# Moving the small score matmuls to the end of a visit that covers two pairs of heads

## The chip, the cores and the metric

The kernel runs on one core of a Trainium2 chip. The metric is the time on the device of one execution, in microseconds (us); of several executions the median is taken. The engines are named as the profile names them: PE (TensorE, its matmuls), PEld (TensorE's loads of stationary weights), DVE (VectorE), ACT (ScalarE), POOL (GpSimd) and SP (SyncE, which here only starts transfers). PSUM has eight banks of 128 partitions by 512 float32 values, and matmuls write there.

## What is computed

Blockwise causal attention over 8 batches, 8 heads, 576 positions and 64 values per head, followed by a feed-forward layer with a swish gate:

```python
block = 64
scores = matmul(q, k.transpose(0, 1, 3, 2)) / sqrt(64)
scores = where(pos[:, None] // block >= pos[None, :] // block, scores, -1e9)
attn = exp(scores - max) / sum
x = matmul(attn, v)              # then reshaped to 4608 rows by 512
h = x @ w_in                     # 512 by 2048
g = h * (1 / (1 + exp(-beta * h)))
out = g @ w_out                  # 2048 by 512
```

A query sees the keys of its own block of 64 positions and of all earlier blocks. In tiles of 128 keys, the scores are a staircase: key tile 0 needs all 576 queries, tile 1 the queries from 128 on, and so on; the last key tile has only 64 keys and the last 64 queries.

## The kernel before

Two heads form a pair, of which there are 32, four to a batch. In a pair, one head's 64 values lie in partitions 0 to 63 and the other's in partitions 64 to 127, so the score matmuls of the two heads use the two row halves of the array and run beside each other. Scores are computed transposed, keys in PSUM's partitions, queries along the free dimension.

The scores of one pair fall into four groups, and the table `blocks` in the function `fq` lists them (key tile, first query, last query, offset in the bank):

- group 0: key tile 0 with queries 0 to 511
- group 1: key tile 0 with the last 64 queries, and key tile 1 with 448 queries
- group 2: key tile 2 with 320 queries, and key tile 3 with 192 queries
- group 3: key tile 4, which has 64 keys and 64 queries: a matmul of 64x64 for each head

Groups 0 to 2 write to a pair of PSUM banks each (tile class `PP`), one bank for each head, with all 128 columns of the array; this is the form 64*128 in the profile. Group 3 writes to partitions 0 to 63 for one head and 64 to 127 for the other, of one shared bank (`small`, of class `P1`), and uses 64 rows by 64 columns of the array for each: the form 64*64.

A *visit* is one operation of the plan in which PE computes some of these groups without a break. For batches 0 and 1 a visit covers one pair of heads. For batches 2 to 7 (`JOIN`), two pairs, `u` and `u + 1`, share three visits: groups 0 and 1 of the first pair; groups 2 and 3 of both; groups 0 and 1 of the second pair. There are twelve visits of the middle kind in a run, with twelve matmuls each. All the work in a visit has one set of waits ahead of it, and its last instruction raises the semaphore that ACT waits for.

After a visit ACT computes the exponentials (L724 for groups 0 to 2, 128x1024 values each; L736 for group 3), DVE clears the upper blocks of the staircase (L730, L732), PE multiplies with the values (L764), DVE normalizes (L776, L783) and the result is transposed to `xT`, by PE for the first batches and by a transposing DMA on SP's queue (L800) for the later ones. Q and K arrive by DMA in `ST`, POOL casts them to bfloat16 in `QKn` (L665), and a second transposing DMA (L672) makes `QKT`, which the visits read.

The feed-forward layer runs on nine chunks of 512 rows: PE multiplies with `w_in` (L1000), ACT takes the tanh (L1010), DVE forms the gate (L1014), and PE multiplies with `w_out`, plainly for the first chunk (L1036) and in seven products of quarters for the others (L921). Filler matmuls (L523, L525) keep PE occupied near the start.

The order on every engine is made before the program is built. A planner, the class `Plan`, simulates the engines with durations that are written at each operation, takes the ready operation with the lowest priority value, assigns buffers and PSUM banks, and writes one fixed queue for each engine; `assign` then derives the semaphore waits. Visits are spread through the feed-forward work in this way. The planner sees a visit as a single operation of fixed duration and doesn't look at the order of the matmuls in it. That order is written out by hand: `fq` walks the list `visits` entry by entry, for each entry its blocks, and for each block the two heads.

Of the kernel before, what the change touches and what calls it, by code (L numbers as in the profile page):

```python
# [359 lines left out]
def bass_blockwise_causal_attn__then__act_swish_beta_kernel(  # L360
# [10 lines left out]
    with es:  # L371
# [66 lines left out]
        def pr(u):  # L438
            b, c = divmod(u, NPAIR)
            return u if b < 1 else 10 * u if b < 2 else 994 + 100 * (b - LAG) + 4.9 * c  # L440
        def again(g, o, i, x):

            return g.add_instruction(mybir.InstMatmult(
                start_tensor_calc=True, stop_tensor_calc=True, tile_size=i.tile_size, tile_position=i.tile_position,
                ldweights=False, name=nc.get_next_instruction_name(), engine=i.engine,
                ins=[g.lower_ap(x), i.ins[1]], outs=[g.lower_ap(o)]))
# [154 lines left out]
        for u in range(NU):  # L601
# [77 lines left out]
            if b not in JOIN or p == 0:  # L679
                tes = {uu: P.tile("EX" if uu == 3 else "E") for uu in ((u,) if b not in JOIN else (u, u + 1))}  # L680
                qks = {uu: {} for uu in tes}
                visits = [[(u, g) for g in grp] for grp in GROUPS[b]] if b not in JOIN else [
                    [(u, 0), (u, 1)], [(u, 2), (u, 3), (u + 1, 2), (u + 1, 3)], [(u + 1, 0), (u + 1, 1)]]
                for grp in visits:
                    small = P.tile("P1") if any(g0 == 3 for _, g0 in grp) else None
                    pst = [P.tile("PP") if g0 < 3 else small for _, g0 in grp]

                    def fq(g, e, pst=pst, grp=grp, tqk=tqk, b=b):
                        keep = {}
                        for (uu, g0), ps in zip(grp, pst):  # L690

                            held = g0 == 1 and (uu, 0) in grp
                            blocks = {0: [(0, 0, 512, 0)], 1: [(0, 512, 576, 448), (1, 128, 576, 0)],
                                      2: [(2, 256, 576, 0), (3, 384, 576, 320)], 3: [(4, 512, 576, 0)]}[g0]
                            for t, q0, q1, off in blocks:
                                m = min(128, 576 - 128 * t)
                                for h in range(2):
                                    r = slice(64 * h, 64 * h + 64)
                                    if g0 < 3:
                                        o = PS[0:m, ps.slot + h, off:off + q1 - q0]  # L700
                                    else:
                                        o = PS[r, ps.slot, 64 * (uu % 2):64 * (uu % 2) + 64]
                                    y = 64 * h * (b >= QB)
                                    x = QKT[tqk.slot][r, uu % 2, 0, q0 + y:q1 + y]
                                    if held and t == 0:
                                        z = again(g, o, keep[h], x)
                                        continue
                                    z = g.matmul(o, QKT[tqk.slot][r, uu % 2, 1, 128 * t + y:128 * t + m + y], x)  # L708
                                    if t == 0:
                                        keep[h] = z.ins  # L710
                        return z

                    n = sum(220 if g0 < 3 else 60 for _, g0 in grp)
                    o = P.op("PE", n, fq, deps=cps, tiles=list({id(x): x for x in pst}.values()) + [tqk] + [tes[uu] for uu in sorted({uu for uu, _ in grp})] * (b > 0),
                             lat=n + 200, mode="row", prio=pr(u) + .2 if len(grp) == 4 else pr(u + 1) + .1 if grp[0][0] > u else
                             pr(u) + .1 + .1 * (grp[0][1] >= 2))
                    for (uu, g0), ps in zip(grp, pst):
                        qks[uu][g0] = o, ps
# [411 lines left out]
```

The softmax here doesn't subtract the row's maximum and nothing guards it: scores larger than these inputs give would overflow.

## Time and profile before

| what | before |
|---|---|
| median of 3 runs | 334.65 us (332.92 to 335.12) |
| span of the profiled execution | 330.9 us |
| the profiled execution's own time around its span | not on the page; median less span is 3.75 us |
| PE busy, of the span | 323.5 us |
| DVE busy / ACT busy | 221.8 us / 212.6 us |
| score matmuls of L708, form 64*128, 320 columns | 64, mean 306 ns |
| score matmuls of L708, form 64*128, 192 columns | 64, mean 243 ns |
| score matmuls of L708, form 64*64, 64 columns | 64, mean 212 ns |
| weight loads of L708, form 64*64 | 64, mean 103 ns |

The span runs from the first to the last instruction. A row of the profile such as "L708 PE MATMUL PS<-QKT 64*128 64x320" gives the line of the kernel, the engine, the operation, the written and the read tile, the rows and columns of the array in use, and the size of the moving operand. Matmuls overlap one another, so the mean duration of a row isn't what the matmul costs PE; the distance from one start to the next is nearer to it. The arrow at the end of a line names what ended the idle time ahead of an instruction.

### The profile page before, as it was taken

How to read it: one execution, taken by the hardware profiler on the slowest of the kernel's cores; microseconds unless marked ns; L12 is line 12 of the kernel's file. 1: busy time of each engine (PE TensorE's matmuls, PEld its weight loads, DVE VectorE, ACT ScalarE, POOL GpSimd, SP SyncE). 2: the span in 40 equal slices, each digit the busy share in tenths (PEclk: the TensorE clock that was granted, in tenths of full speed). 3: DMA queues.
4: the chain of work that ended last, by engine and by line, in shares of the span. 5: the costliest groups of instructions: out<-in, count | busy, mean ns of one | idle time of the engine just before them, and what ended most of it. 6: DMA issues, size and time to landing. Idle time of an engine off the chain costs nothing.

```text
span 330.9 us, 7510 instructions
## 1 busy us (share of the span) xinstructions
PE 323.5 (98%) x3145; PEld 204.2 (62%) x3089; DVE 221.8 (67%) x448; ACT 212.6 (64%) x324; POOL 84.6 (26%) x127
## 2 busy tenths in 40 slices
PE   7998999999999999999999999999999999999996
PEld 4574455445586457754765666576566766666685
DVE  4747875679754897358966695678467685666742
ACT  2876974297558886768657866974975555544521
POOL 7665081073073044104621530320000000000000
PEclk9999999999999999999999999999999999999999
DMA  7999999999999999979999999974102310110023
GB/s 214 229 239 234 192 234 198 187 293 200 202 268 190 207 247 198 229 158 216 204 176 224 199 240 214 200 152 80 35 34 40 92 45 34 60 37 32 3 95 127
DMA packets 154993, 53.41 MB, mean 161 GB/s; under 512 B 139072, under 2 KB 154448, under 8 KB 154960
## 3 DMA queue, kind: packets, MB, share of 16 engines
q1 hardware_dynamic: 141200, 40.19, 63.9%
q0 software_dynamic: 5568, 4.36, 8.3%
q10 hardware_dynamic: 8192, 8.39, 8.1%
q8 instruction: 24, 0.39, 0.5%
q14 instruction: 9, 0.07, 0.1%
HBM read 36.71 MB, written 9.44 MB: 139 GB/s over the span
## 4 chain that ended last, share of the span: by engine, by line
PE 92%; ACT 2%; DMA 2%; issue 1%; DVE 1%; SPq 1%; POOL 0%
PE PS L1000 38%; PE PS L921 30%; PE PS L708 9%; PE PS L764 8%; PE PS L1036 4%; DMA ST<-in_k_dram 2%; PE PS L525 1%; PE PS L813 1%; ACT E L724 1%; PE PS L634 1%; ACT xq L788 1%; SPq L618 1%; ACT th L1010 0%; POOL QKn L625 0%; DVE xq L783 0%
## 5 line engine op out<-in xcount | busy, mean ns | idle before, releaser
L1000 PE MATMUL PS<-xT,w_in 128*128 128x512 bf16 x576 | 136.6, 379 | 0.1
L1010 ACT ACTIVATE th<-PS,beta 128x512 f32<-128x512 f32 x144 | 96.5, 699 | 59.8 <-PE PS L1000 59.1
L1014 DVE SCALAR_TENSOR_TENSOR gT<-th,PS 128x512 f16<-128x512 f32 x144 | 95.1, 681 | 31.7 <-ACT th L1010 31.1
L724 ACT ACTIVATE E<-PS 128x1024 bf16<-128x1024 f32 x93 | 92.1, 1028 | 27.0 <-PE PS L708 27.0
L1000 PEld LDWEIGHTS PS<-xT,w_in 128*128 128x128 bf16 x576 | 53.4, 98 | 55.5 <-DVE gT L1014 1.8
L921 PE MATMUL PS<-w_out,gT 128*128 128x256 f16 x512 | 63.1, 273 | 0.0
L921 PEld LDWEIGHTS PS<-w_out,gT 128*128 128x128 f16 x512 | 49.0, 98 | 12.1 <-issue 1.5
L574 POOL CAST Vn<-Vs 128x640 bf16<-128x640 f32 (+1 forms) x28 | 21.6, 770 | 94.3 <-DMA Vs<-in_v_dram 93.1
L665 POOL CAST QKn<-ST 128x640 bf16<-128x640 f32 x48 | 36.7, 764 | 25.1 <-DMA ST<-in_q_dram 12.9
L708 PE MATMUL PS<-QKT 64*128 64x320 bf16 (+4 forms) x328 | 36.4, 297 | 0.4 <-ACT E L736 0.2
L764 PEld LDWEIGHTS PS<-Vn,E 128*128 128x128 bf16 x930 | 30.9, 97 | 3.9 <-issue 0.4
L942 ACT ACTIVATE ost<-PS 128x512 f32<-128x512 f32 x32 | 19.4, 606 | 21.5 <-PE PS L921 21.5
L921 PE MATMUL PS<-OV 128*128 128x256 f16 x256 | 31.9, 273 | 0.0
L764 PE MATMUL PS<-Vn,E 128*128 128x65 bf16 x930 | 31.8, 193 | 0.0
L708 PEld LDWEIGHTS PS<-QKT 64*128 64x128 bf16 (+1 forms) x328 | 13.4, 96 | 26.4 <-issue 11.6
L921 PEld LDWEIGHTS PS<-OV 128*128 128x128 f16 x256 | 24.2, 98 | 5.8 <-issue 1.1
L783 DVE TENSOR_TENSOR xq<-PS,inv 128x640 bf16<-128x640 f32 x30 | 24.6, 822 | 0.7
L885 DVE TENSOR_TENSOR OV<-gT 128x1024 f16<-128x1024 f16 x32 | 23.8, 753 | 1.1 <-PE PS L921 0.6
L730 DVE MEMSET E<- 64x64 uint32 x62 | 6.9, 112 | 22.5 <-ACT E L724 20.4
L945 DVE SCALAR_TENSOR_TENSOR ost<-PS,ost 128x512 f32<-128x512 f32 x22 | 15.1, 688 | 8.7 <-PE PS L921 6.2
L921 PE MATMUL PS<-OV,gT 128*128 128x256 f16 x128 | 16.1, 273 | 0.0
L1036 PE MATMUL PS<-w_out,gT 128*128 128x512 f16 x64 | 15.5, 380 | 0.0
(65 smaller groups left out, 176.2 us busy)
## 6 DMA issues: line engine op xcount, KB each, us to landing
out_dram<-ost ACTq DMA_DIRECT2D x32, 256.0 KB, 3.8
ST<-in_q_dram SPq DMA_DIRECT2D x12, 576.0 KB, 5.4
ST<-in_k_dram SPq DMA_DIRECT2D x12, 576.0 KB, 7.6
Vs<-in_v_dram SPq DMA_DIRECT2D x24, 256.0 KB, 4.3
ST<-in_q_dram SPq DMA_DIRECT2D x8, 288.0 KB, 6.3
ST<-in_k_dram SPq DMA_DIRECT2D x8, 288.0 KB, 6.5
w_in<-in_moe_w_in_dram POOLq DMA_DIRECT2D x4, 512.0 KB, 10.5
w_out<-in_moe_w_out_dram POOLq DMA_DIRECT2D x4, 512.0 KB, 9.5
```

The source lines that it names most:

```text
L574: return g.tensor_copy(Vn[t.slot][:, 0:n, g0:g1, 0:64], Vs[ts.slot][:, 0:n, g0:g1, :])
L665: return g.tensor_copy(QKn[tn.slot][:].rearrange("p a w n -> p (a w n)")[:, 640 * (2 * a + w):][:, 0:640] .rearrange("p (t h d) -> p t h d ...
L708: z = g.matmul(o, QKT[tqk.slot][r, uu % 2, 1, 128 * t + y:128 * t + m + y], x)
L724: return g.activation(E3[es_(te)][:, g0, :, :], PS[:, ps.slot:ps.slot + 2, :], ACT.Exp, scale=0.125)
L764: z = g.matmul(o, eblk(te, t, i, h), Vn[Tv.slot][:, t, 2 * c + h, 0:65], start=(t == 0), stop=(t == i))
L783: return g.tensor_tensor(xq[xq_(tx)][:].rearrange("p i (h d) -> p h i d", h=2), both(pv, 0, 64), x, ALU.mult)
L885: return P.op("DVE", dve_t(SZ * HC / 2), mk(lambda g: g.tensor_tensor(fo(), fx(), fy(), op)), deps=deps, tiles=tiles, prio=prio)
L921: x = g.matmul(PS[:, pw.slot, HM * w:HM * w + HM], fa()[:, j, 128 * w:128 * w + 128], fb()[:, j, :], start=first and (pair or w == 0) and ...
L1000: z = g.matmul(PS[:, ph.slot, :], w_in[:, c, 128 * j:128 * j + 128], xT[:, c, row % RX:row % RX + RC], start=(c == 0), stop=(c == 3))
L1010: return g.activation(th[tt.slot][:], PS[:, ph.slot, :], ACT.Tanh, scale=beta[:, j:j + 1])
L1014: return g.scalar_tensor_tensor(out=gT[tg.slot][:, j, :], in0=th[tt.slot][:], scalar=1.0, in1=PS[:, ph.slot, :], op0=ALU.add, op1=ALU.mult)
L1036: z = g.matmul(PS[:, po.slot, 0:d1 - d0], gT[tg.slot][:, j, 128 * w:128 * w + 128], w_out[:, j, d0:d1], start=(j == 0), stop=(j == NJ - 1))
```

## The change

In the middle visit of two pairs of heads, the list of groups is put in another order. Before, it goes through groups 2 and 3 of the first pair and then groups 2 and 3 of the second; afterwards through group 2 of both pairs and then group 3 of both. The set of matmuls, the tiles they read and write and the first and last instruction of the visit are unchanged.

```diff
-                    [(u, 0), (u, 1)], [(u, 2), (u, 3), (u + 1, 2), (u + 1, 3)], [(u + 1, 0), (u + 1, 1)]]
+                    [(u, 0), (u, 1)], [(u, 2), (u + 1, 2), (u, 3), (u + 1, 3)], [(u + 1, 0), (u + 1, 1)]]
```

For each visit this turns the sequence of pairs of matmuls (one for each head) from 320, 192, 64x64, 320, 192, 64x64 into 320, 192, 320, 192, 64x64, 64x64. The number 64x64 stands for the form 64*64, the others for the columns of the form 64*128.

## The prediction

> **What bounds the kernel now.** I read the page's head and busy slices first, then the chain that ended last, then three stretches of the span, and then TensorE's (PE's) timeline inside one of the twelve visits that the diff touches.
>
> ```profile
> span 330.9 us, 7510 instructions
> PE 323.5 (98%) x3145; PEld 204.2 (62%) x3089; DVE 221.8 (67%) x448; ACT 212.6 (64%) x324; POOL 84.6 (26%) x127
> PE   7998999999999999999999999999999999999996
> DMA  7999999999999999979999999974102310110023
> PE 92%; ACT 2%; DMA 2%; issue 1%; DVE 1%; SPq 1%; POOL 0%
> ```
>
> PE is busy in every slice, and the chain that ended last runs along PE for 92% of the span. DMA looks as full as PE until about slice 26 (215 us), so whether PE or the transfers set the pace has to be read from the waits. The stretch from 100 to 260 us, which holds ten of the twelve visits (the others start at 76.42 and 90.38), answers it. The columns are the stretch, its length, and the busy time of PE, weight loads, DVE, ACT and POOL:
>
> ```profile
> 60.00:100.00 40.00, 39.81 (x342) 22.68 (x330) 28.38 (x59) 25.71 (x39) 15.71 (x20) 1.00 1.16 231
> 100.00:260.00 160.00, 160.00 (x1622) 100.22 (x1581) 111.64 (x228) 117.20 (x175) 37.36 (x48) 1.00 0.88 168
> ```
>
> From 100 to 260 us PE is busy 160.00 of 160 us at the full granted clock; the next engine, ACT, has 27% to spare. Of PE's waits in the whole span, which sum to 4.3 us, none is for a transfer. So a nanosecond taken off PE's instruction stream there should come off the end.
>
> Busy time says nothing of how well the time is used, since matmuls overlap. Therefore the timeline of the visit at 119.39 us, put together from short windows of it (start, time, engine, line, tiles, count):
>
> ```profile
> 119.39 0.31 PE L708 MATMUL PS<-QKT 64*128 64x320 bf16 x2
> 119.54 0.25 PE L708 MATMUL PS<-QKT 64*128 64x192 bf16 x2
> 119.72 0.22 PE L708 MATMUL PS<-QKT 64*64 64x64 bf16 x2
> 119.72 0.11 PEld L708 LDWEIGHTS PS<-QKT 64*64 64x64 bf16 x2 [0.21 <-issue]
> 119.86 0.11 PEld L708 LDWEIGHTS PS<-QKT 64*128 64x128 bf16 x3
> 120.01 0.24 PE L708 MATMUL PS<-QKT 64*128 64x192 bf16 x2
> 120.19 0.22 PE L708 MATMUL PS<-QKT 64*64 64x64 bf16 x2
> 120.34 0.39 PE L1000 MATMUL PS<-xT,w_in 128*128 128x512 bf16 x1
> ```
>
> Read the starts, not the durations: 119.39, 119.54, 119.72, 119.86 (the second pair of heads' 320-column matmuls start with those loads), 120.01, 120.19, and 120.34 for the next work. The four 64x64 matmuls are short, yet the steps around them are long, and the load of 64x64 weights appears only at 119.72, after a hole of 0.21 us on the load side; nothing is loaded ahead across the change of form.
>
> The same trace shows what a small pair costs where its neighbours have its own form. Early in the span, a 64x64 pair stands between filler matmuls that are 64x64 as well:
>
> ```profile
> 16.85 0.19 PE L708 MATMUL PS<-QKT 64*64 64x64 bf16 x2
> 16.88 0.28 PE L525 MATMUL PS<-identF,identB 64*64 64x256 bf16 x2
> ```
>
> There the successor starts 0.03 us later (29 ns in the records), and its weights are already loading at 16.85.
>
> **What the Trainium skill says.** (1) "TensorEngine Tiling (Array Packing)", Key Properties: a change of tiling mode, as opposed to a change of tile, drains TensorE. The trace agrees and gives the size, about 95 ns, worked out below. (2) The same page, Restrictions under Tile-to-Partition Mapping: column tiling switches off Fast Weight Load. It agrees: a 64x128 weight load is followed by the next of its row half after 15 ns (119.390 to 119.405), while a 64x64 one needs about 29 (16.606 to 16.635). (3) "TensorE: Matmul & The Clock Gate", The mechanism: loads that go to the background weight buffer are pulled ahead of running matmuls. It agrees within one form (load for the 192-column pair at 119.405, under the 320-column pair), not across forms. (4) "Perfetto Trace Analysis", Tensor Engine Instruction: a matmul's end is estimated by the profiler. So I use starts alone.
>
> **The change, part by part.** It swaps two entries of one list. A visit's operation remains one operation with the same waits; its last instruction, which carries the semaphore, is still the second pair of heads' 64x64 matmul. The planner sees the same duration, and in the built program the queues of ACT, DVE, POOL and SP hold the same instructions in the same order; PE differs only inside twelve visits. No DMA, no wait, no instruction is added or removed. What is moved is one 64x64 pair with its two weight loads, past four wide matmuls and their loads.
>
> Rates: back-to-back 512-column matmuls of L1000 start 216 ns apart, 0.42 ns a column. So 320 columns stream in 134 ns, 192 in 81, 64 in 27.
>
> Before, by the records to the nanosecond at 119.39 us: 320 pair 147, 192 pair 174, small pair 149, and again 146, 176, 149 to L1000. Sum 0.94 us; eleven of the twelve visits run 0.94 (one 0.96). Against the rates, 192 to small is 174 - 81 = 93 above, small to wide 149 - 27 = 122 above (98 of switch and 24 of the exposed load: the small matmuls are recorded as 213 ns here, 189 where the load was hidden), and wide 320 is 147 - 134 = 13 above (its load).
>
> After: 320 pair 147; 192 pair to the second 320 pair, same form, load ahead, 81; second 320 pair, 134; second 192 pair to the small form 174; first small pair to the second 29, as at 16.85; second small pair to the next form 149. The exposed load of 24 is counted once in that 149 and is now the first pair's. Sum 714 ns. Saving: 943 - 714 = 229 ns a visit: two switches (93 + 98) and two exposed loads (24 + 13), times 12 = 2.75 us.
>
> Both ends of what isn't seen in this setting: if the second 320 pair still shows its load (+13), the 192 pair an equal one (+12), and the second small pair has to wait for its slow load (+26, as the 29 ns of load come after the first pair's), the visit takes 765 and the saving is 178 ns, 2.1 us in all. If the second small pair costs nothing beside the first, it is 258 ns, 3.1 us. A loss inside the visit I exclude: each step of the new order occurs in the old one or is bounded by one that does.
>
> What lies on the path: all of it, as PE doesn't idle from 100 us on. What becomes late next are the PE operations that arrive with little lead over ACT or DVE. By the semaphore times, ACT begins its exponentials at the end of every visit within 0.02 us, so they move up with it and carry what follows. Three L1000 operations and one L764 have leads of only 0.06, 0.11, 0.16 and 0.13 us over the DVE release they need (219.7, 225.9, 255.2 and 139.9 us). If those releases don't move, 0.17 + 0.12 + 0.07 + 0.10 = 0.46 us is lost there. I take a little under half, 0.2. Transfers: the shortest lead of a transposed Q/K tile is 2.3 us (visit at 175.26, by when seven visits will have saved 1.6); the last xT transposes lead L1000 at 267.15 by 1.4 us, but were issued after PE's own attention product at 261.02, so they move too.
>
> Net 2.55 us: the profiled span goes from 330.9 to about 328.3. Its own time outside the span isn't on the page; the median of the runs, 334.65, is 3.75 above the span, and I carry that over: **332.1 us**, 0.8% less.
>
> **The rivals.**
>
> A, forecast: full saving passed on, 332.1 (331.5 to 332.6 by the bounds). For: no PE idle. Chance 0.70.
>
> B, given back in waits: the visit shortens, but a reader of the small waits is right more often than I am; ACT, at 73% in the stretch, and DVE, at 70%, hold up PE after half the visits. 2.75 / 2 = 1.4 us left, 333.3. For: leads under 0.3 us follow five visits. Against: ACT waits for PE (27.0 us for visits alone), not the reverse. Chance 0.15.
>
> C, the order doesn't matter: the 0.1 us belongs to a small matmul as such, wherever it stands (two row halves writing one PSUM bank, say). Then 334.6. Against: 29 ns at 16.85, and the 64-column pair of L443, 28 ns in the wide form. That the new order isn't made at all is ruled out by the built program. Chance 0.07.
>
> D, slower: PE runs ahead of the transposed Q/K tiles while DMA is full. They take 4.9 to 12.3 us to land, typically 7.0. Should shifted timing turn a typical landing into the longest for a tile with 2.3 us of lead, PE stands 12.3 - 7.0 - 2.3 = 3.0 us; two such make 6.0, less 2.55 gained: +3.5, 338.1. It decides from 2.55 us of such waits in all (5.9 to show as slower). For: the DMA row. Against: eleven of the twelve landings lead by over 3 us, and PE waits for none now. Chance 0.06; 0.02 for others.
>
> **How the numbers follow.** About 1% (3.35 us) is what a measurement of this kernel can tell from no change; the three runs shown spread by 2.2 us. Case A lies within 1%; only its upper bound with the spread in its favour crosses, 0.12 in all. Slower is D. So faster 0.12, same 0.82, slower 0.06. The range takes A's bounds with half the spread of the runs on the low side, 330.9, and reaches over B to 334.0.
>
> **What would show it.** In the visits: starts 0.08 us after the first 192 pair for the second 320 pair, one hole on the load side instead of two, the four small matmuls in one group, a visit of about 0.71 us, the 64x64 row's mean nearer 200 ns than 212. PE still busy 160 of 160 us. Wrong if visits stay at 0.94 (C), if PE shows new waits for ACT or DVE after them (B), or for QKT transposes (D).

## The result: 0.4% less, where 0.8% was forecast

| | before | after |
|---|---|---|
| median of 20 runs | 334.2 us | 332.96 us |
| ratio of after to before | | 0.9959, 95% interval 0.9938 to 0.9981 |
| span of the profiled execution | 330.9 us | 330.6 us |
| its own time | not on record | 332.43 us |

The ratio is a gain of 1.4 us (0.6 to 2.1). The two medians, of all runs, are 1.2 us apart; the ratios, and the means of runs given below, leave out runs that took over 1.5% more than the fastest of their kernel. The time lies in the stated range of 330.9 to 334.0, and within 1% as was thought likeliest. It lies there because that range reached over rival B as well: the forecast itself was a gain of 2.55 us, which is outside the interval of the measured one. The question for the experiments is where the rest is.

The head of the page of the changed kernel, with the lines that answer to those shown of before (the granted clock added):

```profile
span 330.6 us, 7476 instructions
PE 319.7 (97%) x3111; PEld 204.3 (62%) x3089; DVE 221.6 (67%) x448; ACT 212.6 (64%) x324; POOL 85.9 (26%) x127
PE   6897999999999999999999999999999999999996
PEclk9997999999999999999999999999999999999999
PE 89%; ACT 2%; DVE 2%; DMA 2%; issue 2%; SPq 1%; POOL 0%
```

The two spans differ by 0.3 us alone, and it would be wrong to read the change's worth from them: this execution has something that the profiled execution of before has not. In slice 4 (25 to 33 us), long before the first of the twelve visits, PE had less than the full clock. Also, 34 matmuls fewer are on the page than before, all of L1000 (542 of 576): these are missing records. Most are the first of a row of L1000, and there the records show PE idle for 50 to 160 ns. Twenty of them lie between 100 and 260 us, and that is why the stretches (their length, then busy PE, PEld, DVE, ACT, POOL) show 158 us where before had 160:

```profile
60.00:100.00 40.00, 39.82 (x336) 22.77 (x330) 30.49 (x59) 23.76 (x37) 17.36 (x20) 1.00 1.09 229
100.00:260.00 160.00, 158.23 (x1619) 101.41 (x1598) 110.89 (x231) 119.20 (x178) 36.84 (x48) 1.00 0.92 170
```

PE's timeline of the visit that answers to the one shown of before, again put together from short windows:

```profile
121.10 0.31 PE L708 MATMUL PS<-QKT 64*128 64x320 bf16 x2
121.24 0.38 PE L708 MATMUL PS<-QKT 64*128 64x192 bf16 x4
121.33 0.38 PE L708 MATMUL PS<-QKT 64*128 64x320 bf16 x4
121.46 0.39 PE L708 MATMUL PS<-QKT 64*128 64x192 bf16 x4
121.64 0.25 PE L708 MATMUL PS<-QKT 64*64 64x64 bf16 x4
121.64 0.14 PEld L708 LDWEIGHTS PS<-QKT 64*64 64x64 bf16 x4 [0.21 <-issue]
121.82 0.39 PE L1000 MATMUL PS<-xT,w_in 128*128 128x512 bf16 x1
```

(The count in a line is of what overlaps the window, so take starts alone.) The second pair's 320 columns start 0.09 us after the first pair's 192, at 121.33, where a change of form took 0.17. The four small matmuls are one group with one hole of 0.21 us on the load side, not two. The visit runs from 121.10 to 121.82: 0.72 us, where it ran 0.94. The groups of small matmuls and their loads, first of before and then of after (count, then busy time and mean ns of one, then the idle time ahead):

```profile
L708 PE MATMUL PS<-QKT 64*64 64x64 bf16 x64 | 6.9, 212 | 0.0
L708 PEld LDWEIGHTS PS<-QKT 64*64 64x64 bf16 x64 | 3.4, 103 | 6.3 <-issue 6.3
L708 PE MATMUL PS<-QKT 64*64 64x64 bf16 x64 | 4.7, 204 | 0.0
L708 PEld LDWEIGHTS PS<-QKT 64*64 64x64 bf16 x64 | 2.5, 104 | 3.8 <-issue 3.8
```

So inside the visits the change did what was forecast. Two more facts stand in the records of both traces. From one end of a PE operation to the next, by the semaphore that PE raises, after gains on before exactly twelve times by 0.22 us, at the twelve visits, and nowhere from 60 us to the end does it lose more than 0.04. And the first visit begins at 78.73 us in this execution and at 76.42 in the one of before. The whole of the saving, 2.6 us, is in the stretch that the change touches, and 2.3 us were lost ahead of it.

### The profile page after: what moved, and what is told of

Same layout as the page of the kernel before. It is cut to its first block, busy times and chain, and to the rows that moved or that the text cites. A ratio compares the mean times of both kernels' runs of the same rounds, so it can differ in the third digit from the quotient of the medians.

```text
span 330.6 us, 7476 instructions
## 1 busy us (share of the span) xinstructions
PE 319.7 (97%) x3111; PEld 204.3 (62%) x3089; DVE 221.6 (67%) x448; ACT 212.6 (64%) x324; POOL 85.9 (26%) x127
## 4 chain that ended last, share of the span: by engine, by line
PE 89%; ACT 2%; DVE 2%; DMA 2%; issue 2%; SPq 1%; POOL 0%
PE PS L1000 36%; PE PS L921 29%; PE PS L708 8%; PE PS L764 8%; PE PS L1036 4%; DMA ST<-in_k_dram 2%; PE PS L525 1%; PE PS L813 1%; ACT E L724 1%; PE PS L634 1%; DVE gT L1014 1%; ACT xq L788 1%; SPq L618 1%; DVE xq L783 0%; ACT th L1010 0%
## 5 line engine op out<-in xcount | busy, mean ns | idle before, releaser
L1000 PE MATMUL PS<-xT,w_in 128*128 128x512 bf16 x542 | 130.9, 381 | 2.7 <-issue 0.5
L1000 PEld LDWEIGHTS PS<-xT,w_in 128*128 128x128 bf16 x576 | 53.4, 98 | 55.9 <-issue 2.2
L921 PE MATMUL PS<-w_out,gT 128*128 128x256 f16 x512 | 63.0, 273 | 0.0
L921 PEld LDWEIGHTS PS<-w_out,gT 128*128 128x128 f16 x512 | 48.9, 98 | 12.2 <-issue 1.5
L665 POOL CAST QKn<-ST 128x640 bf16<-128x640 f32 x48 | 37.9, 789 | 28.4 <-DMA ST<-in_k_dram 14.9
L708 PE MATMUL PS<-QKT 64*128 64x512 bf16 (+4 forms) x328 | 34.2, 297 | 0.4 <-ACT E L736 0.2
L921 PE MATMUL PS<-OV 128*128 128x256 f16 x256 | 32.0, 273 | 0.0
L921 PEld LDWEIGHTS PS<-OV 128*128 128x128 f16 x256 | 24.2, 98 | 5.7 <-issue 1.1
L885 DVE TENSOR_TENSOR OV<-gT 128x1024 f16<-128x1024 f16 x32 | 23.9, 753 | 1.1 <-PE PS L921 0.6
L921 PE MATMUL PS<-OV,gT 128*128 128x256 f16 x128 | 16.1, 273 | 0.0
L642 DVE COPY QKT<-PS 128x576 bf16<-128x576 bf16 x16 | 12.0, 756 | 5.8 <-PE PS L634 5.6
```

Of the source, the lines that this page charges most:

```text
L665: return g.tensor_copy(QKn[tn.slot][:].rearrange("p a w n -> p (a w n)")[:, 640 * (2 * a + w):][:, 0:640] .rearrange("p (t h d) -> p t h d ...
L885: return P.op("DVE", dve_t(SZ * HC / 2), mk(lambda g: g.tensor_tensor(fo(), fx(), fy(), op)), deps=deps, tiles=tiles, prio=prio)
L921: x = g.matmul(PS[:, pw.slot, HM * w:HM * w + HM], fa()[:, j, 128 * w:128 * w + 128], fb()[:, j, :], start=first and (pair or w == 0) and ...
L1000: z = g.matmul(PS[:, ph.slot, :], w_in[:, c, 128 * j:128 * j + 128], xT[:, c, row % RX:row % RX + RC], start=(c == 0), stop=(c == 3))
```

## The experiments

Two theories were held against each other. **Theory P**: what PE saves in the visits, 2.65 us, passes to the end in full, and what is missing from the medians is scatter ahead of the first visit. **Theory W**: about half is taken back by new waits after the visits. Each kernel was timed in five rounds against the kernel before. For each one profile was taken, and read in three stretches. A visit is measured from its first start to the start of what follows it. Single visits read 0.02 to 0.04 us more than the table has, and one of after's 0.95, by a missing record.

| kernel | visit, us | first visit at | first to last visit | last visit to end | half clock at 28 to 33 us | ratio to before (95%) |
|---|---|---|---|---|---|---|
| before | 0.94 | 76.42 | 173.42 | 81.06 | no | |
| before, copy (e1_null) | 0.94 | 78.56 | 173.39 | 81.07 | yes | 0.9999 (0.998 to 1.0018) |
| before, copy (e9_null) | 0.94 | 78.37 | 173.39 | 81.06 | yes | 1.001 (0.999 to 1.003) |
| after | 0.72 | 78.73 | 171.03 | 80.84 | yes | 0.9959 (0.9938 to 0.9981) |
| after (e2_after) | 0.72 | 78.75 | 171.11 | 80.83 | yes | 0.995 (0.9923 to 0.9976) |
| after (e8_after) | 0.72 | 78.28 | 171.90 | 80.84 | yes | 0.9949 (0.9925 to 0.9973) |
| half the visits (e3_half) | six 0.72, six 0.94 | 76.39 | 172.45 | 81.06 | no | 0.998 (0.9954 to 1.0005) |
| sixteen small pairs more (e4_pad) | 1.23 | 78.61 | 176.51 | 81.34 | yes | 1.01 (1.0061 to 1.0139) |
| small ones first (e5_first) | 0.72 | 79.16 | 171.62 | 80.84 | yes | 0.9984 (0.9962 to 1.0006) |
| six changes of form (e6_six) | 1.05 | 78.00 | 174.56 | 81.16 | yes | 1.0033 (1.001 to 1.0056) |
| after, early fillers (e10_fill_after) | 0.72 | 77.62 | 171.46 | 80.84 | no | 0.9946 (0.9928 to 0.9964) |
| before, early fillers (e11_fill_before) | 0.94 | 77.48 | 176.76 | 81.06 | no | 1.0036 (1.0017 to 1.0056) |

In the diffs below three dots mark lines left out. They are against the changed kernel; that of the six changes of form is against the kernel before, and the fillers went into both.

**The kernel before, copied, twice.** No edit.

> The kernel before, unchanged, against itself. Theory P (what PE saves in the twelve visits reaches the end in full, and the missing half lies in the scatter of the first 76 us, where nothing was changed): the ratio's interval holds 1.000; the stretch from the first of the twelve visits to the last is 173.4 us again within 0.3, while the start of the first visit moves by a microsecond or more against 76.42 us. Theory W (half of the saving is taken back by waits): says nothing of this run but that the first visit starts near 76.4 us again within 0.3, since the stretch before it does not scatter.

> The kernel before a second time, unchanged, beside it. Ratio's interval holds 1.000; the stretch of half clock in about 4 of 10 runs; first visit to last 173.4 us; the first visit near 76.4 us without that stretch in the profile, near 78.6 with it.

Both ratios hold 1.000, the middle stretch is the same to 0.03 us both times, and the first visit moves by 2.1 and 2.0 us. The half clock was in 7 and 8 of 22 runs. So the scatter is ahead of the visits, and the middle stretch is a clean measure of an edit to the visits. The larger part of the move comes with the stretch of half clock. The windows of the first copy's profile (length, busy PE, PEld, DVE, ACT, POOL, then the granted clock):

```profile
24.60:28.05 3.45, 2.04 (x37) 1.62 (x34) 2.79 (x8) 1.68 (x7) 3.23 (x4) 1.00 1.19 213
28.05:31.46 3.41, 3.37 (x20) 1.63 (x19) 1.45 (x2) 0.85 (x3) 1.65 (x2) 0.50 1.19 251
```

For 3.41 us PE runs at 0.50 of its clock, after a stretch in which it was busy 2.04 us of 3.45. In every profile with this stretch the first visit starts between 78.0 and 79.2 us, and in the two without it or the early fillers at 76.4. By the ends of PE's operations against those of before, 1.2 to 1.4 us of each move arise from 27 us on, with the half clock; up to 0.8 us had arisen in the first 15 us, and up to 0.8 us at a hole of PE near 26 us, of which more below. The Trainium skill, "TensorE: Matmul & The Clock Gate", What's actually happening, tells of a gate that halves PE's clock by what it saw in free-running windows of 3413 ns; the record's 3.41 us at 0.50 agrees. The page puts the half clock after an idle window; the 3.45 us ahead of it here were busy for 2.04, so what brings it here is not shown.

**The changed kernel, again, twice.** No edit to it.

> The changed kernel again, unchanged. Theory P: visits of 0.72 us; first visit to last 171.0 us, 2.4 less than before's 173.4; the end 2.2 to 2.9 us earlier than before on average over enough runs (ratio 0.991 to 0.9935), if it is not the first stretch that is longer for a reason. Theory W: ratio 0.995 to 0.997 again, and PE waits on ACT, DVE or DMA after the visits that before does not have, about 1.3 us in all.

> The changed kernel a third time, for how often its runs have the stretch of half clock at 28 to 33 us, so far in 28 of 39 runs, against 30 of 78 of before. If that is the change's doing: again in about 7 of 10. If it is chance: nearer to before's 4 of 10. Theory P: among runs with the full clock throughout, 2.3 to 2.65 us below before. Theory W: 1.3 us.

The visits take 0.72 us again, and the gain is 1.7 us both times (ratios 0.995 and 0.9949): in the runs, what theory W expected and less than theory P did. In the first of the two the middle stretch is 171.11, and there is one loss, of 0.12 us. In the second it is 171.90, and 0.93 us is lost at three places, two of which the waits of PE from 60 us on name (who waited for whom: us, times, longest):

```profile
PE PS L1000 <- DVE gT L1014: 0.2, 1, 0.2
PE PS L921 <- DVE OV L885: 0.2, 1, 0.2
PE PS L708 <- ACT E L724: 0.2, 1, 0.2
```

The last line is in every kernel's profile, before's too. The first two are in none of the kernels whose visits are as long as before or longer; nor are they in e2_after's (after's list has the first, at missing records). What happened at the first place, in the timeline of the same run:

```profile
79.80 1.84 POOL L665 CAST QKn<-ST 128x640 bf16<-128x640 f32 x2 [1.18 <-DMA ST<-in_k_dram]
79.99 1.07 DVE L885 TENSOR_TENSOR gT<-gT 128x1024 f16<-128x1024 f16 x1
81.34 0.84 DVE L885 TENSOR_TENSOR OV<-gT 128x1024 f16<-128x1024 f16 x1
82.47 1.28 DVE L1014 SCALAR_TENSOR_TENSOR gT<-th,PS 128x512 f16<-128x512 f32 x2
83.81 1.04 PE L1000 MATMUL PS<-xT,w_in 128*128 128x512 bf16 x4 [0.23 <-DVE gT L1014]
```

And the same operations in the kernel before:

```profile
78.12 0.75 DVE L885 TENSOR_TENSOR gT<-gT 128x1024 f16<-128x1024 f16 x1
79.15 0.69 DVE L885 TENSOR_TENSOR OV<-gT 128x1024 f16<-128x1024 f16 x1
80.24 1.28 DVE L1014 SCALAR_TENSOR_TENSOR gT<-th,PS 128x512 f16<-128x512 f32 x2 [0.15 <-ACT th L1010]
81.77 1.02 PE L1000 MATMUL PS<-xT,w_in 128*128 128x512 bf16 x4
```

DVE's sum of L885 took 1.07 us rather than 0.75, because it met a cast of POOL, and the cast starts when a transfer lands. DVE's gate work then comes late, and PE stands, 0.40 us by the ends of its operations. In before the release came 0.24 us ahead of PE's need here (its lead), and the shorter visit has spent 0.22 of that; in no profile does PE start here less than 0.06 us after the release. This isn't a single case: in the twelve profiles no L885 sum that is clear of casts takes over 0.70 us, and of those that overlap one for more than 0.1 us some take up to 1.24. Which starts first decides. Where the sum did (38 cases), it took 0.68 to 0.69 us. Where the cast did and the sum took over 0.70 (167 cases), the sum ended 0.54 us after the cast, within 0.01. The Trainium skill, "SBUF — State Buffer", SBUF: two separate sides, says that a DVE instruction with two inputs in SBUF (the memory of all tiles here but `PS`) and a GpSimd instruction that reads SBUF lock a pair of ports against each other, the first to start for its whole length; these sums agree. The second place, near 200 us, is of the same kind: L885 sums of 1.20 and 1.09 us beside casts, then PE's L921 stands, 0.39 us, where it had 0.61 us of lead in before. The third, 0.14 us at L1000, follows a wait for transposed `xT`.

In how many runs is the half clock? With the mean granted clock of each run (0.995 or less with it, 0.999 or more without): 13 of 20, 15 of 19 and 13 of 22 runs of the changed kernel, 41 of 61. Of the kernel before and its copies, 78 of 215. Since it costs 1.4 us (among before's runs in the comparisons, means of 333.7 without it and 335.1 with it), this difference in share is worth 0.4 us of the missing gain. Without it throughout, the changed kernel's 20 runs in the comparisons have a mean of 332.1: 1.6 us below before, not 2.6. Of the second repeat this number had been foretold, 2.3 to 2.65 us by theory P and 1.3 by theory W; it is 1.4 (332.3 in 9 runs, 333.7 in 44 of before), so here W's number came. Its share of runs with the half clock, 13 of 22, lies between the two that were to tell the change's doing from chance.

**The new order in half of the visits.**

```diff
-                    [(u, 0), (u, 1)], [(u, 2), (u + 1, 2), (u, 3), (u + 1, 3)], [(u + 1, 0), (u + 1, 1)]]
+                    [(u, 0), (u, 1)], ([(u, 2), (u + 1, 2), (u, 3), (u + 1, 3)] if b < 5 else [(u, 2), (u, 3), (u + 1, 2), (u + 1, 3)]), [(u + 1, 0), (u + 1, 1)]]
```

> The new order in the six visits of batches 2 to 4 alone, the old order in batches 5 to 7. Visits of 0.72 and of 0.94 us. Theory P: 1.33 us earlier than before (ratio 0.996). Theory W: 0.6 us or less (0.998).

Six visits take 0.72 and six 0.94. The ratio is 0.998, 0.7 us less, between the two theories and unable to part them. The profile does better: six steps of -0.22, and one loss of 0.37 us at the place shown above, by the same meeting of L885 (1.04 us) and a cast. From the first visit to the last it gains 0.96 us, not the 1.3 of its six steps.

**PE time added to the visits.** The last small pair is issued sixteen times more, with the same operands to the same place.

```diff
-                        return z
+                        return again_small(g, PS, QKT[tqk.slot], pst[-1].slot, grp[-1][0] % 2, 16) if len(grp) == 4 else z
...
+def again_small(g, PS, x, slot, a, n):
+    for h in [0, 1] * n:
+        r, k = slice(64 * h, 64 * h + 64), slice(512 + 64 * h, 576 + 64 * h)
+        z = g.matmul(PS[r, slot, 64 * a:64 * a + 64], x[r, a, 1, k], x[r, a, 0, k])
+    return z
```

> The new order, with the last pair of small matmuls issued sixteen times more in each of the twelve visits (same result, same place), 29 ns a pair: PE's time in a visit goes from 0.72 to about 1.18 us, 5.6 us more over the run. This measures at which rate PE's time in these visits reaches the end. Theory P: all of it, 5.6 us over the changed kernel, 2.9 us over before (ratio to before 1.0085). Theory W: half, 2.8 us over the changed kernel, 1.5 us over before (1.0045).

The visits take 1.23 us, 0.506 more than in the changed kernel (sixteen pairs at 32 ns), 0.285 more than in before. Against before, twelve steps of +0.28 or +0.29 us reach the end and nothing over 0.04 us is given or taken elsewhere: first to last visit +3.10 for eleven steps. The ratio of the six runs agrees: theory W's 1.0045 lies below its interval. So PE's time in these visits goes to the end at a rate of one when it gets longer, and theory W is wrong as a rate. It is right only for the direction in which PE gets ahead of the others.

**The small matmuls first.**

```diff
-                    [(u, 0), (u, 1)], [(u, 2), (u + 1, 2), (u, 3), (u + 1, 3)], [(u + 1, 0), (u + 1, 1)]]
+                    [(u, 0), (u, 1)], [(u, 3), (u + 1, 3), (u, 2), (u + 1, 2)], [(u + 1, 0), (u + 1, 1)]]
```

> In the twelve visits the four small matmuls run first, ahead of both pairs' wide blocks: as many changes of form as in the changed kernel (three), in other places. If the changes of form are what is paid for: visits of 0.72 us, the same step of -0.22 us at each visit against before, first visit to last 171.1 us, end as the changed kernel (ratio 0.993 to 0.997). If the place at the end of the visit matters (the semaphore after a short matmul, say): visits other than 0.72 us by more than 0.03.

Visits of 0.72 us, as many changes of form as in the changed kernel: the place doesn't matter inside a visit. The ratio, 0.9984, is worse than the changed kernel's by more than expected. The profile shows eleven steps of -0.22 and one of -0.11, and losses of 0.34 us (the place shown above, L885 at 1.01 us beside casts) and 0.20 (the one near 200 us, L885 at 1.20). Whether the order itself brings more such meetings, or this one series of runs did, isn't decided.

**More changes of form.** The small pair stands between its pair of heads' 320 and 192 columns.

```diff
-                        for (uu, g0), ps in zip(grp, pst):
+                        for (uu, g0), ps, part in cut(grp, pst):
...
-                                      2: [(2, 256, 576, 0), (3, 384, 576, 320)], 3: [(4, 512, 576, 0)]}[g0]
+                                      2: [(2, 256, 576, 0), (3, 384, 576, 320)], 3: [(4, 512, 576, 0)]}[g0][part]
...
+def cut(grp, pst):
+    if len(grp) < 4:
+        return [(x, ps, slice(None)) for x, ps in zip(grp, pst)]
+    return [(grp[i], pst[i], p) for a in (0, 2) for i, p in ((a, slice(0, 1)), (a + 1, slice(None)), (a, slice(1, 2)))]
```

> Each small pair stands between the 320 and the 192 columns of its own pair of heads: six changes of form where before has five and the changed kernel three. If changes of form are paid for: 1.05 us a visit (before 0.943: one more switch of 93 to 98 and a load of 13), first visit to last 174.6 us, end 1.3 us later than before (ratio 1.004). If a small pair costs what it costs wherever it stands: 0.94 us and a ratio of 1.000.

1.049 us a visit, twelve steps of +0.11 us, and 1.0033: all as the price of a change of form says. With the same matmuls, three changes give 0.72, five 0.94, six 1.05 us, counting the ones into and out of the visit. That a small pair costs the same wherever it stands is refuted.

This profile also tests the account of the waits. At the first place shown above its two L885 sums take 0.40 us more than in before, nearly as in e5_first (0.41), again beside casts. Here, where the visit is 0.11 us longer, PE loses nothing over 0.04 us; in e5_first it loses 0.34.

**Without the half clock.** Fillers at the head of one early transpose operation, in both kernels.

```diff
-                for i in range(5):
+                for i in filled(g, tx.cls == "XX", PS[:, px.slot, 0:256], identB[:], identW):
...
+def filled(g, here, o, w, x):
+    for _ in range(11 if here else 0):
+        g.matmul(o, w, x)
+    return range(5)
```

> The changed kernel with eleven filler matmuls of 256 columns (1.2 us) at the head of one early transpose operation of PE (L813, the fourth pair of heads), where PE stands 1.1 to 1.3 us near 26 us in every profile before its fifth transpose goes out. Theory that the stretch of half clock comes from that hole: its share of runs falls from 6 in 10 to near none, and the first visit starts near 76.4 us or up to 1.2 us later if the hole isn't hidden. If it does not: 6 in 10 again. Against the kernel before, if the fill costs nothing itself: 2 to 2.6 us less.

> The kernel before with the same fillers, beside it. With the half clock gone from both, the pair shows the change alone. Theory P: 2.3 to 2.65 us between the two. Theory W, in the form that profiles now show (PE stands up to 0.9 us in a run where DVE's quarter sums of L885 meet casts of POOL): 1.7 to 2.3 us between the two.

The fillers don't fill the hole. It moves: PE issues four of the eleven and stands 0.9 to 1.0 us ahead of the other seven, where before it stood ahead of the fifth transpose. In PE's stream it has not moved at all: in all twelve profiles it comes after 349 matmuls, fillers counted, and the last transfer of instructions ahead of its end (16384 bytes, of the kind that the profile calls instruction) has landed 1.3 to 1.6 us before that end. This points to the supply of instructions: then work put ahead of the hole can't fill it. In both profiles the fillers cost 1.1 us. In the runs at the full clock they cost 1.1 us in the old order (334.8 for 333.7), but only 0.1 in the new one (332.2 for the 332.1 above), and why isn't known. In the runs of this series the half clock is rare in all three: 5 of 20, 5 of 22, and 9 of 40 of before. So it is not shown that the hole causes it, nor that the change does; its share differs between series too.

But the pair is the cleanest comparison of the two orders: medians of 332.38 and 334.94, 2.56 us apart. Among the runs at the full clock in the comparison, means of 332.17 (15 runs) and 334.82 (17 runs) are 2.65 apart. The standard deviations, 0.63 and 0.72 us, put some 0.5 us on either side. This is theory P's value, though the profile of the first also has the loss of 0.41 us at the place shown. But the 1.6 us between the two orders without fillers, also known to some 0.5, is not reconciled with it. In the profile of the second, an execution of the old order, PE stands from 171.7 to 174.6 us for a transposing transfer, the kind of wait that rival D of the prediction was about (here of `xT`). Near 88 us it also waits for `QKT` itself, D's own wait:

```profile
PE PS L1000 <- DMA xT<-xq: 2.9, 1, 2.9
PE PS L708 <- DMA QKT<-QKn: 0.2, 1, 0.2
```

These two make its 176.76 us from first to last visit; the first shows what such a landing costs when it is late, and that it needs no shorter visits to happen.

## Why the prediction was right and wrong

**Change of form, right.** The saving of 229 ns a visit was measured as 221, and the twelve visits as 2.65 us for 2.75. The order 320, 192, 320, 192 costs 147, 83, 135 and 176 ns from start to start. The small pairs were in sum 3 ns off (181 for 178) though not in their parts: the second starts 52 ns after the first, near the upper bound that was stated (29 + 26), after the first's load and then its own. The step from 192 columns to the small form, taken as 174 ns, is 176 in the records of before too, as its 943 needs; this puts that change of form at 95 ns.

**All of it on the path, right in the trace, not in the medians.** That PE's saved time passes on was shown by steps of 0.22 us that stay to the end, and in the other direction by e4_pad and e6_six. The step that was mis-sized is "I take a little under half, 0.2", the part that is lost in waits. The profiles of the new order show 0, 0.12 and 0.93 us lost, and those of its relatives 0.37 (half of the visits), 0.48 and 0.54. None of it is at the four places that the prediction named by their leads of 0.06 to 0.16 us. The two places that lose most have leads of 0.24 and 0.61 us in before. A lead read from one execution was taken for a fixed quantity; but DVE's sums vary from 0.68 to 1.24 us with the casts that they meet, and the casts follow transfers, which need not move with PE (at the first place PE was 1.6 us later in e8_after than in before, the cast 0.4). Where PE runs late, as in e6_six, the lead absorbs that; where the visit gives it 0.22 us, as in e5_first, it doesn't.

**Rival B, nearer to the measured time.** It gave 333.3 for a chance of 0.15, and 332.96 came. Its mechanism, PE held up by DVE, is what the traces show; that this is after half of the visits is not: it is at no more than three places in a profile. And the waits seen are on the average less than B's half of the saving.

**The time around the span, wrong.** It was taken as 3.75 us, the median less the span. For the profiled execution of after it is 332.43 less 330.6, 1.8 us. Then the profiled execution of before took about 332.7 us: it was one of the short ones, at the full clock throughout. The sum, being a difference, was not touched by it. The lower end of the range doesn't come out as described: A's 331.5 less half of the spread is 330.4, not 330.9.

**Rivals C and D.** C, no effect of the order, is refuted by the visits. D did not come as a loss of the changed kernel; its wait for `QKT` was seen once, for 0.2 us, in the old order with fillers.

**What stays open.** The gain in the ratios of three series is 1.4 to 1.7 us. Of the missing 0.9 to 1.3, the waits seen in the profiles account for 0.35 on the average of three (0, 0.12, 0.93), and the larger share of runs with the half clock for about 0.4. The rest is within the scatter. At the full clock alone, where the share plays no part, 1.0 us is missing, with 0.5 on either side; the waits cover a third of that, and the rest is not explained. Why more runs of the changed kernel had the half clock, 50 us ahead of the first instruction that differs, isn't known; half-changed and padded kernels had it in 12 of 22 and 4 of 6, that with the small ones first in 13 of 22, that with six changes of form, whose visits are longer, in 12 of 22, and the filled one no more often than before. So a shorter visit is not what these have in common.

## What to carry to other kernels

Count the changes of tile form in PE's instruction stream, not the small matmuls: here each cost 93 to 98 ns of PE and an exposed weight load of 13 to 24, and ordering by form took away two at no other cost. On PE, which was busy for 160.00 of 160 us here, the saving went to the end in full until it had eaten the leads of the waits behind it; read these leads together with how much the releasing instruction varies between executions. To see what an edit is worth, compare the stretch that it touches, step by step, since 2 us of scatter ahead of that stretch hide a change of 1%.

## What the runs showed of the hardware

A 64x64 pair followed by another takes 52 to 53 ns from start to start when the first had to load after a change of form, and 32 ns in a long row of such pairs. The hole of PE near 26 us, which the profile puts down to issue, lasted 1.1 to 2.0 us in the ten profiles without early fillers and 0.9 to 1.0 in the two with them; in all twelve it came after the same 349 matmuls of PE's stream, shortly after a transfer of instructions. A DVE sum of two operands in SBUF took 0.68 to 0.69 us clear of POOL's casts or when it began ahead of one, and ended 0.54 us after the cast's end when the cast had begun first, up to 1.24 us in all.
